# New orders for every engine of a two-layer linear-attention and MLP kernel, with the same operations

## The chip, the core and the metric

The kernel runs on one NeuronCore of a Trainium2 chip. The core has five engines with an instruction queue each: TensorE (PE, matmuls), VectorE (DVE), ScalarE (ACT), GpSimd (POOL) and SyncE (SP, which here only issues DMAs). An engine works its queue off in order; between engines there are semaphores. The metric is the time on the device for one execution, in microseconds (us).

## The reference

The input is x, 2048 tokens of 512 features in bfloat16. One set of weights is used twice, in two layers. A layer is a linear attention of 32 heads of 16 features, and then an MLP of 1792 hidden features with its own inner layer norm:

```
phi = lambda t: jnp.where(t > 0, t + 1, jnp.exp(t)) + 1e-6
pq, pk = phi(q), phi(k)
kv = jnp.einsum("bhsd,bhse->bhde", pk, v)
z = jnp.einsum("bhsd->bhd", pk)
num = jnp.einsum("bhqd,bhde->bhqe", pq, kv)
den = jnp.einsum("bhqd,bhd->bhq", pq, z)[..., None] + 1e-6
...
x = x + _A_ref(_layernorm(x, axis=-1), A_wqkv, A_wo)
x = x + _B_ref(_layernorm(x, axis=-1), B_w1, B_b1, B_w2, B_b2)
x = x + _A_ref(_layernorm(x, axis=-1), A_wqkv, A_wo)
x = x + _B_ref(_layernorm(x, axis=-1), B_w1, B_b1, B_w2, B_b2)
```

`_A_ref` is num / den times wo; `_B_ref` normalizes once more, multiplies by w1, adds b1, applies gelu, multiplies by w2 and adds b2. All tokens' keys are needed before the first token's attention is known, since kv and z are sums over the sequence.

## The kernel before, in words

The tokens are cut into four chunks c of four tiles k of 128 tokens; st = 4c + k numbers the tiles, L the layers. `build_kernel` does not issue instructions: it records operations into a graph (`G.op`), each with a name, an engine, and what it reads and writes. Names carry layer and tile. The ones that matter here:

- loads: x0 and x1 (first chunk), xc1, xc2, xc3 (the others), wka to wkd and wq (parts of the weights); b2 loads the bias of the second MLP matmul for all partitions.
- layer norm of tile st before the attention (A) or the MLP (B): statsA0_st and aggr (DVE), veps (one small operation, DVE or POOL), pow (POOL: the reciprocal root), norm (DVE, or ACT, which also takes nmr on POOL). The normalized tile is transposed: TA0_st, TB0_st are DMA transposes on SP's queue (L812); PTA0_2 and PTA0_3 are done by TensorE (L825) and copied by ACT (tcA0_2, tcA0_3, L835).
- K0_st, Q0_c_k: key and query matmuls (L879, L896, L909), four instructions each. phi of them: exp and relu on ACT, min on DVE, and the sum phi on DVE or POOL.
- G0_st: the running sum of y-transposed times phi(k) over tiles (L984 in layer 0, L1013 in layer 1); Z and zs, zb, ZR: the sum z. KV, kvm, M, cpm: the sum times wv, masked to its heads, times wo.
- Dividing by den: D, ln, rec, pr for chunk 0; for the others pz (query times z, L1077), red, den, rec, pr (L1089), and then TP0_c_k, a DMA transpose (L1093).
- WO0_st: the attention's output matmul (L1123); RA0_st adds the residual (DVE, L1128); b20_st adds the MLP's output bias to the residual ahead of time (L1139).
- W10_c_ft_h: the first MLP matmul for 128 hidden features (L1153), on 512 tokens, or in chunk 0 in two halves of 256; gelu0_c_ft_h on ACT (L1158). W20_st_0 and W20_st_7: the second MLP matmul in two parts of seven instructions (L1190); RB0_st adds the residual (L1196, or L1200 in the last layer, where OD stores the tile).
- warm0 to warm8: matmuls on ones ahead of the first real work (L749), 7 of 512 and 8 of 256 columns.

Layer 1 has the same names with 1 for 0. What runs when is not decided by a scheduler at build time: `CONF["ORDER"]` lists, for each engine, all its operations by name in the order in which they are issued, and `CONF["PLACES"]` says which buffer every tile has and who has it after whom (eight PSUM banks, and rings of SBUF buffers). `CONF["WAY"]` chooses the engine where there is a choice. `Settled` replays these lists, and `assign_waits` puts in the semaphore waits that the dependencies need: an operation waits for what it reads, and for the last user of the buffer that it takes over.

Of the kernel before, what the change touches and what calls it, by code (L numbers as in the profile page):

```python
# [185 lines left out]
def assign_waits(graph, order, sems, dma_sems):  # L186
# [10 lines left out]
    while len(done) < total:  # L197
        moved = False
        for e in ENGINES:
# [43 lines left out]
    LOADS=[['x0', 'sp', 'x', 0, 0, 1, ''], ['x1', 'sp', 'x', 0, 1, 4, ''], ['wkb', 'act', 'wk', 0, 2, 3, 'ones'], ['wka', 'sp', 'wk', 0, 0, 1, ''], ['wkd', 'act', 'wk', 0, 3, 4, ''], ['wkc', 'sp', 'wk', 0, 1, 2, ''], ['xc1', 'sp', 'x', 1, 0, 4, 'x0'], ['wq', 'sp', 'wq', 0, 0, 4, ''], ['xc3', 'sp', 'x', 3, 0, 4, ''], ['xc2', 'sp', 'x', 2, 0, 4, '']],  # L243
    ORDER={
        "sp":
            "x0 x1 wka wkc xc1 wq xc3 TA0_0 TA0_1 xc2 TA0_5 TA0_4 TA0_7 TA0_6 TA0_13 TA0_14 TA0_15 TA0_12 TA0_8 TA0_10 TA0_9 "
            "TA0_11 b1 Tb1 TP0_1_3 b2 TP0_1_1 TP0_1_0 TP0_1_2 TB0_0 TB0_1 TB0_2 TB0_3 TB0_7 TP0_2_1 TB0_5 TB0_4 TB0_6 TP0_2_2 "
            "TP0_2_0 TP0_2_3 TP0_3_2 TP0_3_0 TP0_3_1 TB0_10 TA1_0 TP0_3_3 TB0_8 TB0_9 TB0_11 TA1_1 TB0_12 TB0_14 TB0_15 "
            "TB0_13 TA1_2 TA1_3 TA1_7 TA1_4 TA1_6 TA1_5 TA1_9 TA1_8 TA1_11 TA1_10 TA1_13 TA1_12 TA1_15 TA1_14 TP1_1_2 TP1_1_0 "
            "TP1_1_1 TB1_0 TB1_1 TB1_2 TB1_3 TP1_1_3 TP1_3_1 TB1_6 TB1_4 TB1_5 TB1_7 TP1_3_3 TP1_2_1 TP1_3_0 TP1_3_2 TB1_13 "  # L250
# [3 lines left out]
            "warm0 warm8 warm2 warm6 PTC0 warm1 warm7 warm5 warm4 warm3 K0_0a K0_0b PTC1 K0_0c K0_0d PTA0_2 K0_1 PTA0_3 K0_2 "  # L254
            "K0_3 G0_0_0 G0_1_0 Q0_0_2 Q0_0_1 Q0_0_0 K0_5 G0_2_0 K0_4 Z0_0 G0_3_0 Q0_1_0 K0_7 Q0_1_3 K0_6 G0_4_0 G0_5_0 "
            "Q0_1_2 K0_13 K0_14 G0_6_0 K0_12 Z0_1 K0_15 K0_10 K0_8 K0_9 K0_11 G0_7_0 Q0_1_1 Z0_3 Q0_0_3 Z0_2 G0_8_0 G0_9_0 "
            "D0_0_2 G0_10_0 D0_0_0 G0_11_0 ZR0 D0_0_3 G0_12_0 G0_13_0 G0_14_0 G0_15_2 G0_15_1 G0_15_0 D0_0_1 Q0_3_3 G0_15_3 "
            "Q0_2_0 KV0_0 KV0_1 KV0_2 KV0_3 Q0_2_1 M0_2 M0_0 M0_1 Q0_2_2 M0_3 Q0_2_3 WO0_0_0 WO0_0_1 WO0_0_2 WO0_0_3 WO0_1_0 "
            "Q0_3_0 WO0_2_0 WO0_3_0 Q0_3_1 WO0_7_0 Q0_3_2 WO0_4_0 WO0_6_0 WO0_5_0 W10_0_3_0 W10_0_6_0 W10_0_1_0 W10_0_4_0 "
            "W10_0_0_0 W10_0_8_0 W10_0_12_0 W10_0_2_0 W10_0_7_0 W10_0_13_0 W10_0_5_0 W10_0_11_0 W10_0_9_0 W20_1_0 W10_0_10_0 "  # L260
            "W20_0_0 W10_0_9_1 W10_0_2_1 W10_0_4_1 W10_0_12_1 W20_0_7 W20_1_7 W10_0_6_1 W10_0_10_1 W10_0_8_1 W10_0_11_1 "
            "W10_0_1_1 WO0_9_0 W10_0_13_1 W10_0_5_1 W10_1_3_0 W10_1_9_0 W10_1_8_0 W10_1_2_0 W10_1_13_0 W10_0_7_1 W10_1_5_0 "
            "W10_1_1_0 W10_1_12_0 W10_1_4_0 W10_1_7_0 WO0_10_0 W10_1_0_0 W10_1_10_0 W10_0_0_1 W10_1_11_0 W10_1_6_0 WO0_8_0 "
            "WO0_11_0 W20_4_0 W20_7_0 W20_4_7 W20_7_7 W20_6_0 WO0_14_0 W10_0_3_1 WO0_12_0 W20_5_0 W20_6_7 WO0_13_0 K1_0 "
            "W20_5_7 WO0_15_0 W20_2_0 W20_2_7 W10_2_3_0 W10_2_10_0 W10_2_11_0 W10_2_0_0 W10_2_5_0 W20_3_0 W10_2_12_0 "
            "W10_2_4_0 W10_2_1_0 W20_3_7 W10_2_2_0 W10_2_6_0 W10_2_7_0 W10_2_13_0 W10_3_6_0 W20_10_0 K1_1 W10_3_7_0 W10_2_8_0 "
            "W10_3_13_0 W10_3_11_0 W10_2_9_0 W10_3_4_0 W10_3_9_0 W20_9_0 W20_9_7 K1_7 K1_2 K1_3 W10_3_5_0 W20_8_0 W20_10_7 "
            "W20_8_7 W10_3_12_0 W10_3_1_0 K1_6 W10_3_3_0 W20_11_0 W10_3_0_0 K1_4 K1_5 G1_0_3 W20_11_7 W10_3_2_0 W10_3_10_0 "
            "G1_0_1 G1_0_2 W10_3_8_0 G1_0_0 K1_9 W20_13_0 K1_8 W20_12_0 Q1_1_0 W20_12_7 W20_13_7 W20_14_0 W20_14_7 K1_11 "
            "K1_10 W20_15_0 W20_15_7 G1_1_3 G1_1_1 G1_1_0 G1_1_2 Q1_1_1 Q1_1_2 Q1_0_0 K1_12 K1_13 K1_15 K1_14 Q1_1_3 ZH "  # L270
            "G1_2_1 G1_2_2 Q1_0_3 Z1_3 Q1_0_2 Q1_0_1 G1_3_1 ZR1 D1_0_0 G1_3_2 G1_2_3 G1_2_0 D1_0_2 D1_0_1 G1_3_0 G1_3_3 "
            "Q1_3_1 D1_0_3 Q1_3_2 KV1_0 KV1_1 KV1_2 KV1_3 Q1_3_0 M1_2 M1_0 M1_1 M1_3 Q1_2_0 WO1_0_0 WO1_0_1 WO1_0_2 WO1_0_3 "
            "WO1_1_0 Q1_3_3 WO1_2_0 WO1_3_0 Q1_2_1 Q1_2_3 Q1_2_2 WO1_6_0 WO1_5_0 WO1_4_0 W11_0_12_0 W11_0_11_0 W11_0_6_0 "
            "W11_0_8_0 W11_0_2_0 W11_0_7_0 W11_0_1_0 W11_0_0_0 W11_0_10_0 W11_0_4_0 W11_0_9_0 W11_0_13_0 W11_0_5_0 W11_0_3_0 "
            "W11_0_0_1 W11_0_12_1 W11_0_6_1 W11_0_1_1 W11_0_5_1 W11_0_11_1 W11_0_4_1 W11_0_7_1 W11_0_8_1 W11_0_10_1 "
            "W11_0_13_1 WO1_7_0 W11_0_9_1 W11_0_3_1 W11_0_2_1 W21_0_0 W21_3_0 WO1_13_0 W21_0_7 W21_2_0 W21_2_7 W21_1_0 "
            "W21_1_7 WO1_15_0 W21_3_7 W11_1_12_0 W11_1_5_0 W11_1_1_0 WO1_9_0 W11_1_10_0 W11_1_6_0 W11_1_13_0 W11_1_2_0 "
# [12 lines left out]
            "expq0_2_0 ln0_0_1 rec0_0_1 cpm0_0 cpm0_1 cpm0_3 reluq0_3_3 expq0_3_3 expq0_2_2 expq0_2_1 expq0_2_3 reluq0_2_2 "  # L290
            "reluq0_2_1 expq0_3_0 b1c reluq0_2_3 reluq0_3_0 gelu0_0_6_0 gelu0_0_3_0 gelu0_0_1_0 gelu0_0_0_0 gelu0_0_8_0 "
            "gelu0_0_4_0 gelu0_0_12_0 gelu0_0_7_0 gelu0_0_2_0 gelu0_0_5_0 reluq0_3_1 gelu0_0_13_0 normB0_7 gelu0_0_9_0 "
            "gelu0_0_10_0 gelu0_0_11_0 expq0_3_1 expq0_3_2 normB0_6 gelu0_0_9_1 gelu0_0_4_1 gelu0_0_12_1 gelu0_0_6_1 "
            "gelu0_0_10_1 gelu0_0_2_1 gelu0_0_8_1 gelu0_0_11_1 gelu0_0_13_1 gelu0_0_5_1 gelu0_1_3_0 gelu0_1_9_0 gelu0_1_8_0 "
            "gelu0_0_1_1 gelu0_1_13_0 gelu0_0_7_1 gelu0_1_5_0 gelu0_1_1_0 gelu0_1_12_0 gelu0_1_2_0 gelu0_1_7_0 gelu0_1_4_0 "
            "gelu0_0_0_1 gelu0_1_0_0 gelu0_1_11_0 gelu0_1_10_0 gelu0_1_6_0 gelu0_0_3_1 normB0_11 normB0_9 expk1_0 reluk1_0 "
            "gelu0_2_10_0 gelu0_2_3_0 gelu0_2_5_0 gelu0_2_11_0 gelu0_2_12_0 gelu0_2_4_0 gelu0_2_0_0 gelu0_2_2_0 gelu0_2_6_0 "
            "gelu0_2_1_0 gelu0_2_13_0 gelu0_3_6_0 normA1_2 gelu0_3_7_0 gelu0_2_7_0 gelu0_3_13_0 gelu0_3_11_0 gelu0_2_8_0 "
            "normA1_7 gelu0_2_9_0 gelu0_3_4_0 expk1_2 expk1_7 expk1_3 normA1_6 reluk1_2 expk1_1 reluk1_3 normA1_5 gelu0_3_9_0 "
            "gelu0_3_5_0 gelu0_3_12_0 gelu0_3_3_0 gelu0_3_1_0 reluk1_6 expk1_6 reluk1_4 expk1_5 expk1_4 reluk1_7 normA1_9 "  # L300
            "gelu0_3_10_0 gelu0_3_2_0 gelu0_3_0_0 normA1_11 gelu0_3_8_0 expk1_8 normA1_10 reluk1_9 expk1_9 reluk1_8 expq1_1_0 "
# [1058 lines left out]
```

## Time and profile before

| | us |
|---|---|
| time, median of 3 runs | 323.07 (322.53 to 324.76) |
| time of the profiled execution | 323.1 |
| its span, first to last instruction | 321.9 |
| TensorE busy | 318.0 |
| DVE busy | 218.1 |
| ACT busy | 189.3 |
| POOL busy | 145.5 |

The table's lower half is from the profiled execution: the span is what the profiler saw of the program's instructions, and the execution took 1.2 us more than that. Busy times are unions of an engine's instructions. A matmul's end is modelled: a 512-column matmul is shown as 379 ns, while the next one of a row of such starts 216 ns after it, so that TensorE's pace is read from starts. DMAs belong to no engine's busy time; their landing is told by semaphores. "Margin" in this document means the time from the end of the last thing that an operation waits for to its start.

### The profile page before, as it was taken

The numbers are of one execution on the slowest core, as the hardware profiler recorded it, in microseconds if no ns is written. First come the engines' busy times: TensorE is split into PE (matmuls) and PEld (weight loads), VectorE is DVE, ScalarE is ACT, GpSimd is POOL, SyncE is SP. The second block draws the span as 40 slices with busy tenths as digits, with TensorE's granted clock in tenths as the row PEclk, the third lists the DMA queues.
The fourth block names the chain that finished last, engine by engine and source line by source line (L and its number), as shares of the span: only waits on it lengthen the run. The fifth ranks groups of instructions, "written<-read, shape, count | busy, mean of one in ns | idle before, by whom it ended". The sixth has DMA issues, their size and how long they took to land.

```text
span 321.9 us, 4748 instructions
## 1 busy us (share of the span) xinstructions
PE 318.0 (99%) x1703; PEld 157.4 (49%) x1703; DVE 218.1 (68%) x529; ACT 189.3 (59%) x324; POOL 145.5 (45%) x216
## 2 busy tenths in 40 slices
PE   8999999999999999999999999999999999999997
PEld 3444554666444444444444444558544444444444
DVE  5998789999786774028848899999889881101103
ACT  5898656797730636667962367979634442663320
POOL 6573978688655355101822415887454163000000
DMA  7844793142121412111010200122232322201002
GB/s 257 200 81 85 241 348 85 35 82 36 33 49 34 82 33 51 34 33 32 18 40 10 51 16 0 35 51 52 50 62 54 98 65 67 49 0 35 16 33 65
DMA packets 52355, 21.68 MB, mean 67 GB/s; under 512 B 47532, under 2 KB 50860, under 8 KB 52332
## 3 DMA queue, kind: packets, MB, share of 16 engines
q1 hardware_dynamic: 50844, 16.37, 22.4%
q0 software_dynamic: 1056, 4.72, 4.3%
q10 hardware_dynamic: 432, 0.30, 0.3%
q8 instruction: 13, 0.21, 0.3%
q14 instruction: 10, 0.08, 0.1%
HBM read 8.00 MB, written 2.10 MB: 31 GB/s over the span
## 4 chain that ended last, share of the span: by engine, by line
PE 97%; DMA 2%; DVE 0%; issue 0%
PE ps L1153 30%; PE ps L1190 29%; PE ps L1123 9%; PE ps L879 8%; PE ps L896 6%; PE ps L984 4%; PE ps L1013 4%; DMA t<-in_A_x_dram 2%; PE ps L909 2%; PE ps L1176 1%; PE ps L970 1%; PE ps L1034 1%; PE ps L1057 1%; PE ps L1100 1%; DVE stats L775 0%; PE ps L1048 0%
## 5 line engine op out<-in xcount | busy, mean ns | idle before, releaser
L1158 ACT ACTIVATE gT<-ps,b1c 128x512 bf16<-128x512 f32 (+1 forms) x140 | 77.0, 601 | 68.7 <-PE ps L1153 68.1
L1153 PE MATMUL ps<-t,w 128*128 128x512 bf16 (+1 forms) x560 | 102.5, 336 | 0.0
L1190 PE MATMUL ps<-w,gT 128*128 128x512 bf16 x434 | 98.6, 379 | 0.0
L1153 PEld LDWEIGHTS ps<-t,w 128*128 128x128 bf16 x560 | 54.8, 98 | 43.7 <-ACT gT L1158 0.2
L1190 PEld LDWEIGHTS ps<-w,gT 128*128 128x128 bf16 x434 | 42.5, 98 | 50.4
L784 POOL TENSOR_TENSOR rstd<-veps,neghalf 128x1 f32<-128x1 f32 x64 | 39.0, 625 | 41.1 <-DVE veps L782 38.9
L847 ACT ACTIVATE eb<-ps 128x512 bf16<-128x512 f32 x62 | 35.4, 606 | 19.3 <-PE ps L896 7.3
L1200 DVE TENSOR_TENSOR yb<-ps,xsb 128x512 bf16<-128x512 f32 x15 | 10.2, 688 | 41.4 <-PE ps L1190 41.4
L775 DVE BATCH_NORM_STATS2 stats<-xsb 128x6 f32<-128x512 f32 x48 | 32.0, 681 | 0.3
L1123 PE MATMUL ps<-gtb,t 128*128 128x512 bf16 x128 | 31.4, 379 | 0.0
L879 PE MATMUL ps<-wqkv,t 128*128 128x512 bf16 x128 | 30.9, 379 | 0.3 <-ACT t L835 0.3
L858 ACT ACTIVATE rb<-ps 128x512 bf16<-128x512 f32 x43 | 25.3, 607 | 5.8 <-PE ps L879 5.8
L798 ACT ACTIVATE yb<-xsb,nmr,rstd 128x512 bf16<-128x512 f32 x21 | 16.9, 814 | 15.1 <-POOL nmr L795 15.1
L896 PE MATMUL ps<-wqkv,t 128*128 128x512 bf16 x96 | 24.1, 379 | 0.0
L1089 POOL TENSOR_TENSOR t<-t,rr 128x512 bf16<-128x512 bf16 x18 | 19.3, 1072 | 9.0 <-DVE rr L1085 6.4
L782 POOL TENSOR_SCALAR veps<-mv 128x1 f32<-128x1 f32 x35 | 8.2, 236 | 32.7 <-DVE mv L777 31.3
L1196 DVE TENSOR_TENSOR xsb<-ps,xsb 128x512 f32<-128x512 f32 x16 | 10.8, 678 | 17.9 <-PE ps L1190 17.9
L1139 POOL TENSOR_TENSOR xsb<-xsb,b2b 128x512 f32<-128x512 f32 x17 | 21.4, 1267 | 3.0 <-DVE yb L803 2.9
L1077 POOL TENSOR_TENSOR lr<-t,zrow 128x512 f32<-128x512 bf16 x14 | 16.5, 1179 | 7.3 <-ACT zrow L997 4.5
L1123 PEld LDWEIGHTS ps<-gtb,t 128*128 128x128 bf16 x128 | 12.5, 98 | 14.5
L803 DVE TENSOR_SCALAR yb<-xsb,mv,rstd 128x512 bf16<-128x512 f32 x27 | 14.5, 542 | 7.3 <-POOL rstd L784 6.0
L879 PEld LDWEIGHTS ps<-wqkv,t 128*128 128x128 bf16 x128 | 12.1, 98 | 14.7 <-ACT t L835 0.9
(99 smaller groups left out, 363.7 us busy)
## 6 DMA issues: line engine op xcount, KB each, us to landing
w<-in_B_w_dram POOLq DMA_DIRECT2D x4, 896.0 KB, 9.1
out_dram<-yb SPq DMA_DIRECT2D x15, 128.0 KB, 2.0
t<-in_A_x_dram SPq DMA_DIRECT2D x3, 512.0 KB, 4.8
t<-yb SPq DMA_TRANSPOSE x62, 2.5
wqkv<-in_A_wqkv_dram SPq DMA_DIRECT2D x1, 512.0 KB, 5.9
wqkv<-in_A_wqkv_dram POOLq DMA_DIRECT2D x1, 512.0 KB, 4.7
wo<-in_A_wo_dram POOLq DMA_DIRECT2D x1, 512.0 KB, 5.3
t<-in_A_x_dram SPq DMA_DIRECT2D x1, 384.0 KB, 3.3
```

Source lines behind the costliest of these rows:

```text
L775: G.op("dve", lambda e: e.bn_stats(stats[:, s.slot, :], src()), 620, reads=src_keys, writes=[k + "s"], tiles=[s, *src_tiles], name=f"stats ...
L784: G.op("pool", lambda e: e.tensor_tensor(rstd[:, s.slot:s.slot + 1], veps[:, s.slot:s.slot + 1], neghalf[:], op=ALU.pow), 570, reads=[k + ...
L847: G.op("act", lambda e: e.activation(eb[:, et.slot, :], bank(bt), ACT.Exp, scale=by()), 478, reads=[src_key, *more_keys], writes=[f"e{tag} ...
L858: G.op("act", lambda e: e.activation(rb[:, rt.slot, :], bank(bt), ACT.Relu, scale=by()), 478, reads=[src_key, *more_keys], writes=[f"r{tag ...
L879: ins = e.matmul(bank(b), lhsT=yTa(yT)[:, dt, k * P:(k + 1) * P], rhs=wqkv[:, dt, D:2 * D], start=(i == 0 and n == 0), stop=(i == len(part ...
L896: ins = e.matmul(bank(b), lhsT=yTa(yT)[:, dt, k * P:(k + 1) * P], rhs=wqkv[:, dt, 0:D], start=(dt == 0), stop=(dt == DT - 1))
L1089: lambda e, d=d, tok=tok, heads=heads: e.tensor_tensor(heads(tok()), heads(tok()), rr[:, d.slot, :].unsqueeze(2).broadcast_to([P, H, DH]), ...
L1123: ins = e.matmul(bank(wb), lhsT=yTa(pq)[:, kt, k * P:(k + 1) * P], rhs=gtb[:, kt, :], start=(kt == 0), stop=(kt == DT - 1))
L1139: G.op("pool" if on_pool else "dve", lambda e: e.tensor_tensor(xsb[:, st, :], xsb[:, st, :], b2b[:], op=ALU.add), 1120 if on_pool else 600 ...
L1153: ins = e.matmul(bank(b, n), lhsT=w1[:, dt, ft * P:(ft + 1) * P], rhs=yTa(yT)[:, dt, k0 * P:k1 * P], start=(dt == 0), stop=(dt == DT - 1))
L1158: G.op("act", lambda e, ft=ft, b=b, k0=k0, k1=k1, n=n: e.activation(gT[:, g.slot, ft * 512 + k0 * P:ft * 512 + k1 * P], bank(b, n), ACT.Ge ...
L1190: ins = e.matmul(bank(b), lhsT=gT[:, g.slot, ft * 512 + k * P:ft * 512 + (k + 1) * P], rhs=w2[:, ft, :], start=(ft == 0), stop=(ft == FT - 1))
```

## The change

All five lists of `ORDER` are new, with `PLACES` to match, and 50 entries of `WAY`, each of which sends a small operation to the other one of DVE and POOL. Loads, warm-up matmuls and all operations are the same; TensorE, ACT and SP have the same operations in another order (389, 311 and 113 of them). DVE has 543 instead of 529 and POOL 198 instead of 212. The change was described as orders chosen anew "under a wide spread of the head's landings", that is of the times at which the first loads arrive, with "instruction packets placed by counting TensorE's instructions": the choice of the orders took into account where the DMA packets fall that bring in instructions. Neither of the two shows in the program except in the orders.

The first part of the lists, before (-) and after (+):

```diff
         "sp":
-            "x0 x1 wka wkc xc1 wq xc3 TA0_0 TA0_1 xc2 TA0_5 TA0_4 TA0_7 TA0_6 TA0_13 TA0_14 TA0_15 TA0_12 TA0_8 TA0_10 TA0_9 "
-            "TA0_11 b1 Tb1 TP0_1_3 b2 TP0_1_1 TP0_1_0 TP0_1_2 TB0_0 TB0_1 TB0_2 TB0_3 TB0_7 TP0_2_1 TB0_5 TB0_4 TB0_6 TP0_2_2 "
+            "x0 x1 wka wkc xc1 wq xc3 TA0_0 TA0_1 TA0_5 TA0_4 xc2 TA0_7 TA0_6 TA0_13 TA0_14 TA0_12 TA0_15 TA0_8 TA0_10 TA0_9 "
+            "TA0_11 b1 Tb1 TP0_1_3 TP0_1_1 TP0_1_0 TP0_1_2 TB0_0 TB0_1 TB0_2 b2 TB0_3 TB0_7 TB0_5 TB0_6 TB0_4 TP0_2_1 TP0_2_2 "
...
         "pe":
-            "warm0 warm8 warm2 warm6 PTC0 warm1 warm7 warm5 warm4 warm3 K0_0a K0_0b PTC1 K0_0c K0_0d PTA0_2 K0_1 PTA0_3 K0_2 "
-            "K0_3 G0_0_0 G0_1_0 Q0_0_2 Q0_0_1 Q0_0_0 K0_5 G0_2_0 K0_4 Z0_0 G0_3_0 Q0_1_0 K0_7 Q0_1_3 K0_6 G0_4_0 G0_5_0 "
+            "warm0 warm6 PTC0 warm1 warm7 warm4 warm8 warm3 warm5 warm2 K0_0a K0_0b PTC1 K0_0c K0_0d PTA0_2 K0_1 K0_2 PTA0_3 "
+            "G0_0_0 K0_3 G0_1_0 Q0_0_1 Q0_0_0 K0_5 Q0_0_2 K0_4 G0_2_0 Q0_1_0 G0_3_0 K0_7 G0_4_0 Q0_1_3 G0_5_0 K0_6 Z0_0 K0_13 "
...
         "act":
-            "wkb wkd sumA0_3 tcC0 sqA0_3 tcC1 reluk0_0 tcA0_2 expk0_0 tcA0_3 expk0_1 reluk0_1 reluk0_3 expk0_2 reluk0_2 "
+            "wkb wkd sumA0_3 tcC0 sqA0_3 tcC1 expk0_0 tcA0_2 reluk0_0 expk0_1 reluk0_1 tcA0_3 expk0_2 reluk0_3 reluk0_2 "
```

The change also adds to `CONF` one line, the order of the chunks, which is the old one, and rewrites the functions that took the chunks in their natural order to take it from there. A third way to divide by den (half of a chunk by features, half by tokens) and a half-tile load come into the code, but no entry of `WAY` or `LOADS` asks for them:

```diff
+    CHUNKS=[[0, 1, 2, 3], [0, 1, 2, 3], [0, 1, 2, 3]],
...
-        def by_token(L, c):
-            return eng(f"den{L}_{c}") == "tok"
+        def by_token(L, c, k=0):
+            way = eng(f"den{L}_{c}")
+            return way == "tok" or (way == "half" and k >= 2)
...
-        def mlp_up(L, c, yT, g):
+        def mlp_up(L, c, yT, g, first):
-            parts = [(0, 2), (2, 4)] if c == 0 else [(0, 4)]
+            parts = [(0, 2), (2, 4)] if first else [(0, 4)]
```

From WO1_9_0 on, 244.6 us into the run before, TensorE's list is the old one; ACT's, DVE's, POOL's and SP's follow from about the same point.

Of the 50 operations that change engines, these go from POOL to DVE: pz0_3_0, pz0_3_2, pz1_3_0, pz1_3_1; b20_0, b20_3, b20_4, b20_6, b20_8, b20_11, b20_13, b21_1; pr0_2_0, pr0_2_2, pr0_3_2, pr1_1_2, pr1_3_3; za3, za9; and 13 veps. From DVE to POOL go pz0_2_0, pz1_2_2, pz1_3_2, pz1_3_3; pr0_2_3, pr1_3_0; b21_0; za2, za8, za10; and 8 veps.

## The prediction

> **What bounds the kernel now.** I read the page first: its busy times and the shares of the chain that ended last.
>
> ```profile
> span 321.9 us, 4748 instructions
> PE 318.0 (99%) x1703; PEld 157.4 (49%) x1703; DVE 218.1 (68%) x529; ACT 189.3 (59%) x324; POOL 145.5 (45%) x216
> ...
> PE 97%; DMA 2%; DVE 0%; issue 0%
> ```
>
> TensorE is the bound, and everything else is late only if TensorE sees it. So the second view is who TensorE waited for, over the whole span:
>
> ```profile
> PE ps L749 <- PEq L1345: 0.8, 1, 0.8
> PE ps L825 <- DVE yb L803: 0.5, 1, 0.5
> PE ps L879 <- ACT t L835: 0.3, 1, 0.3
> PE ps L825 <- DVE yb L789: 0.2, 1, 0.2
> ```
>
> That is 1.8 us in all, every bit of it before 9.4 us. Going through TensorE's instructions one by one, 512-column matmuls start 0.216 us apart (eight take 1.73 us in the chain) and 256-column ones 0.109 us apart, without a gap from 9.39 to 319.70 us. So there is nothing to win behind the head. Ahead of it only warm-up matmuls run (0.83 to 4.61 us, until the first x tile has landed and been centred), and behind it stand the last DVE add and store (319.9 to 321.9). The third view is TensorE's timeline in the head:
>
> ```profile
> 7.67 1.03 PE L879 MATMUL ps<-wqkv,t 128*128 128x512 bf16 x4
> 9.16 0.40 PE L825 MATMUL ps<-idp,yb 128*128 128x128 bf16 x4 [0.47 <-DVE yb L803]
> 9.39 1.89 PE L879 MATMUL ps<-wqkv,t 128*128 128x512 bf16 x8
> 11.12 1.89 PE L984 MATMUL ps<-pkb,yb 128*128 128x512 bf16 x8
> ```
>
> The transpose at 9.16 (PTA0_3) stands in the queue ahead of K0_2, whose operand was ready at 8.65: 0.63 us are lost there.
>
> The margins behind the head are thin, though. I set each TensorE operation's start against the end of the last thing it needs: 66 of them have under 0.5 us (a gelu freeing a PSUM bank leaves 0.20 us again and again). The old order has no stall, but a new one with the same work can have some.
>
> **The change, part by part.** Every TensorE, ACT and SP operation stays, with its engine, and warm-up and loads too. 211 of TensorE's 389 places change, 203 of ACT's 311, 36 of SP's 113. 32 small operations go from POOL to DVE and 18 from DVE to POOL.
>
> (1) *The head.* Durations are those of the old rows, 0.06 us from an end to the waiter's start. Now K0_2 stands ahead of PTA0_3: it starts when tcA0_2 is done (8.65), at 8.71, issues until 9.57, and PTA0_3 follows at once until 9.80. G0_0_0 now stands ahead of K0_3 and needs phik0_0, done at 10.74 in the old run. It comes sooner: on ACT expk0_0 now precedes tcA0_2 (7.48 to 8.17), reluk0_0 follows (8.53 to 9.2); on DVE mink0_0 moves ahead of normA0_3 (8.70), normA0_3 ends 9.4, phik0_0 at 9.77. So G0_0_0 9.83 to 10.69. K0_3 needs tcA0_3, now behind expk0_1 and reluk0_1 on ACT (10.06 to 10.68): 10.74 to 11.60. G0_1_0 needs phik0_1 (11.36, behind normA0_5): 11.60 to 12.45. In the old run G0_1_0's last issue ended at 12.85. So **-0.40 us**. Bounds: -0.63 (that wait gone and nothing new) and +0.53 (phik0_0 no sooner than 10.74, then three operations of 0.86 from 10.80). I take -0.40, as each term is a row.
>
> (2) *The next loads.* SP now sends TA0_5 and TA0_4 ahead of xc2. In the old run TA0_5, sent 0.7 us behind xc2, took 3.70 us, and landed 15.14. Now it goes at 11.04 and lands near 13.5 (2.5 us, as the undisturbed ones), for K0_5 at 14.18; TA0_4 near 14.9 for K0_4 at 15.9. xc2 is sent some 2.5 us later and lands near 17.5, and statsA0_8, its first reader, stands on DVE at about 17.8. Its transpose leaves after 25 in both. Nothing is lost: 0.
>
> (3) *Instruction packets.* Transposes in this kernel land 2.4 to 2.5 us after their issue, save a few. The view of the transposing line from 16 to 24 us, and of the queues from 17 to 22 us:
>
> ```profile
> DMA to landing us min/median/max: 2.4/2.5/4.1
> ...
> q8 instruction: 1, 0.02, 1.6%
> q14 instruction: 1, 0.01, 1.0%
> ```
>
> The 4.1 is TA0_6 (17.70 to 21.76): a 16 KB packet of queue 8 began at 18.05 and took 1.26 us. The same befell TA1_13 (4.01, packet at 179.04) and TP1_3_0 (4.02, packet at 243.26); an 8 KB packet of queue 14 cost TB1_0 and TB1_2 0.85 us each. So a hit costs a transpose 1.55 or 0.85 us. There are 13 queue-8 packets, 110 to 149 matmuls apart; TensorE's instructions keep their number, so by that count they stay where they are to within the 0.4 us of (1). TA0_6 is hit again, sent at about 16.8 and landing near 20.9; its reader K0_6 moved from 21.89 (margin 0.13 in the old run) to 22.8. TB0_1 landed at 59.50, and a packet began at 59.56; DVE's minq0_2_2 leaves its way, so it is no later. W10_1 starts at 76.1 instead of 78.3, but its transposes lose TP0_2_1 from between them, the last lands near 73.9. I take 0; a hit without cover is at most +1.55.
>
> The Trainium skill, "Runtime: NRT & Kernel Launch", section "Instruction fetch mechanics", says that instructions come in 16 KiB blocks of 256 by a DMA queue and that crossing a block is mostly hidden. By that the term would be 0 wherever packets fall; the rows agree on the size and show 1.55 us on three transposes.
>
> (4) *DVE from 64 to 96 us.* Nine wide operations come to DVE here (b20_0, _3, _4, _6, pz0_3_0, pz0_3_2, pr0_2_0, pr0_2_2, pr0_3_2) and two wide and two small ones leave: 7 x 0.69 - 0.28 = +4.55 us. DVE has 32.00 - 27.84 = 4.16 us free there:
>
> ```profile
> 64.00:72.00 8.00, 8.00 (x60) 5.54 (x58) 7.51 (x19) 7.41 (x15) 6.99 (x11) 1.00 0.40 82
> 72.00:80.00 8.00, 8.00 (x52) 4.99 (x51) 7.93 (x16) 6.28 (x13) 6.56 (x5) 1.00 0.20 36
> 80.00:88.00 8.00, 8.00 (x40) 3.82 (x39) 6.27 (x15) 5.92 (x11) 5.47 (x6) 1.00 0.16 33
> 88.00:96.00 8.00, 8.00 (x41) 3.83 (x40) 6.14 (x17) 3.61 (x7) 3.95 (x5) 1.00 0.24 49
> ```
>
> (The third busy time is DVE's.) Adding the rows up in the new order from normB0_5 at 68.47: RB0_0 ends 77.9 (WO0_9 needs its bank at 80.9), pr0_2_2 80.2 (with its transpose 82.7; WO0_10 at 85.6), pr0_2_0 86.7 (89.1; WO0_8 at 92.1). Tight is RA0_8, which frees the bank of W20_7_0, due at 95.34: with three long rows of the old run kept (1.30, 0.97 and 1.56 us from start to next start) RA0_8 ends at 95.66, +0.37; with 0.65 for each it ends at 93.9 as before, 0. Taken: **+0.20**, as POOL has less to do beside it.
>
> (5) *Start of layer 1's MLP.* pr1_1_2 comes to DVE ahead of RA1_0, but fills 205.9 to 206.6, and RA1_0 waits for WO1_0_3 until 206.65 anyway. vepsB1_1 goes to POOL, 0.24 instead of 0.15, so TB1_1 is about 0.1 later of the 0.57 that W11_0 has. 0; +0.4 if the 8 KB packet (0.85) hits TB1_1 instead of TB1_0. From WO1_9_0 on (244.6 us) TensorE's list is the old one: 0.
>
> Sum: 323.1 (profiled execution: span 321.9 and 1.2 around it; the median is 323.07, the same) - 0.40 + 0.20 = **322.9 us**.
>
> **Rivals.**
> A, the forecast: 322.9. Own range 322.2 (-0.63, and the 0.3 by which runs lie lower) to 324.4 (+0.53, +0.37, +0.4).
> B, thin margins become waits: one place hit by a packet without cover, as TB0_1 would be if 0.1 us later (1.55 - 0.96 of margin = 0.6), and a gelu chain or two (0.2 to 0.5 each): +1.5, 324.4. For it: the 66 margins; against it: the old order had the same and no stall.
> C, slower than before: DVE's two-input operations blocked by POOL's.
>
> ```profile
> 74.22 2.61 DVE L1077 TENSOR_TENSOR lr<-t,zrow 128x512 f32<-128x512 bf16 x2
> ...
> 79.27 1.37 DVE L1139 TENSOR_TENSOR xsb<-xsb,b2b 128x512 f32<-128x512 f32 x1
> ```
>
> Both stand beside POOL's b20 additions; alone they take 0.68. A blocked one costs up to 0.97. RA0_8 can lose 1.4 us before W20_7_0 waits. Five of the nine moved ones blocked: 4.85 - 1.4 = +3.4, 326.3. The Trainium skill, "SBUF — State Buffer", section "Who interferes with whom", says that a DVE instruction with two SBUF inputs and a GpSimd one that reads SBUF shut each other out for a whole instruction; the trace agrees for these two. Against C: of the 32 DVE operations of these three kinds 5 were long (0.98 to 1.64), and POOL has nine fewer to collide with.
> D, the clock: matmuls start 0.427 us apart until 4.2 us and 0.216 after 4.84. Two of three warm-ups ahead of PTC0 move behind it, so TensorE idles 0.63 instead of 0.15 us there. If the doubling came later, eight matmuls of K0_0 and K0_1 would cost 0.21 more each, half of it in waits: +0.8, 323.7. The Trainium skill, "TensorE: Matmul & The Clock Gate", section "What's actually happening", has a free-running window of 3413 ns of activity; no run here shows its threshold.
>
> **How the numbers follow.** Chances: A 0.66, B 0.20, C 0.07, D 0.07. Range 322.2 to 325.4, which leaves out C and the ends of A and B. One per cent (3.2 us) is about what a measurement of this kernel can tell. Faster by more would need 3.2 us, and all of TensorE's waits are 1.8: 0.01. Slower by more is C and B's far end: 0.08. Within: 0.91.
>
> **What would show it.** Step 1: G0_1_0's last issue near 12.45 and no wait before PTA0_3. Step 3: long transposes only at TA0_6, TA1_13, TP1_3_0 or others with no TensorE wait behind. Step 4: DVE full from 64 to 96, W20_7_0 on time. TensorE's waits should again be under 2.5 us in all. I am wrong if waits for ACT's gelu or DMA stand in that list behind 10 us.

## The result and the profile after

The changed kernel is slower: a median of 324.59 us (324.01 to 326.01) against 323.41 us (322.53 to 325.58) for the kernel before, 17 executions each, ratio 1.0043 with a 95% interval of 1.0030 to 1.0056. That is 1.4 us (1.0 to 1.8) by the ratio and 1.2 by the medians, inside the predicted range and on the other side of the forecast: slower, where faster was forecast. The profiled execution took 324.15 us (323.1 before), its span 322.9 (321.9).

The page of the changed kernel, with the lines that stand against those of before:

```profile
span 322.9 us, 4718 instructions
...
PE 317.3 (98%) x1673; PEld 157.2 (49%) x1703; DVE 224.1 (69%) x543; ACT 191.2 (59%) x326; POOL 132.4 (41%) x202
...
PE 84%; DVE 9%; ACT 2%; POOL 2%; issue 1%; DMA 1%; SPq 0%
```

TensorE is still the bound, but the chain that ended last now runs through DVE for 9% of the span: somewhere TensorE waited for DVE. (30 of its 1703 matmul records are missing, one every 10.8 us; a gap of exactly one matmul's pace is such a record and no idle time.) The whole list of TensorE's waits says where:

```profile
PE ps L759 <- PEq L1373: 0.8, 1, 0.8
PE ps L841 <- DVE yb L805: 0.4, 1, 0.4
PE ps L1149 <- DVE xsb L1154: 0.4, 1, 0.4
PE ps L1216 <- DVE veps L798: 0.3, 1, 0.3
```

The first two stand in the head. The third and fourth are new and stand at 54.8 and 234.7 us. The list counts from the modelled end of the matmul ahead, and the next one could have started before that end; so I take idle time from matmul starts: 0.52 us ahead of WO0_2_0 (plus 0.05 ahead of WO0_3_0), 0.41 ahead of W21_2_0, and 0.14 and 0.04 ahead of W11_0_9_0 and W11_0_13_0, which the list doesn't have. In all 1.17 us behind the head; the kernel before had none in its profile.

**First wait, 54.8 us.** DVE's timeline in the changed kernel (start, duration, line and operation; L867 is the min, the old L851):

```profile
49.92 0.32 DVE L1126 TENSOR_SCALAR rd<-rd 128x32 f32<-128x32 f32 x1
50.15 1.21 DVE L867 TENSOR_SCALAR eb<-eb 128x512 bf16<-128x512 bf16 x1
51.28 0.34 DVE L1128 RECIPROCAL rr<-rd 128x32 f32<-128x32 f32 x1
51.55 0.62 DVE L869 SCALAR_TENSOR_TENSOR t<-ps,eb 128x512 bf16<-128x512 f32 x1
```

and POOL's timeline in the changed kernel at that time:

```profile
49.03 1.17 POOL L1102 TENSOR_TENSOR t<-t,lr 128x512 bf16<-128x512 bf16 x1
50.15 1.06 POOL L1132 TENSOR_TENSOR t<-t,rr 128x512 bf16<-128x512 bf16 x1
```

minq0_2_0 took 1.21 us instead of 0.28: it ended 0.15 us after POOL's pr0_1_1, which began in the same moment. In the kernel before the min came first. DVE's line of it, and POOL's pr0_1_1:

```profile
50.36 0.28 DVE L851 TENSOR_SCALAR eb<-eb 128x512 bf16<-128x512 bf16 x1
50.41 1.14 POOL L1089 TENSOR_TENSOR t<-t,rr 128x512 bf16<-128x512 bf16 x1
```

Behind the min RA0_1 ended at 54.78 instead of 54.11, and WO0_2_0, which in the new `PLACES` takes the bank that RA0_1 frees, was due at 54.32.

**The wait at 234.7 us**, the last in order of time. DVE's timeline of the changed kernel again; L819 is normB1_5 (0.54 before), the last line RA1_13, whose bank W21_2_0 takes (the veps of the list begins beside it and is not what TensorE needs):

```profile
232.35 1.44 DVE L819 TENSOR_SCALAR yb<-xsb,mv,rstd 128x512 bf16<-128x512 f32 x1
233.72 0.34 DVE L1128 RECIPROCAL rr<-rd 128x32 f32<-128x32 f32 x1
233.98 0.62 DVE L1154 TENSOR_TENSOR xsb<-ps,xsb 128x512 f32<-128x512 f32 x1
```

POOL's pz1_2_2, which the change took from DVE, ran from 232.36 to 233.51. W21_2_0 takes RA1_13's bank in the kernel before too; there RA1_13 ended at 232.99 and W21_2_0 began at 233.60.

**The wait at 215.7 us**, between the other two in time. Here POOL is the one shut out. nmrB1_1 in POOL's timeline of the changed kernel (0.65 in the kernel before, 0.27 in the median of its kind):

```profile
211.28 1.09 POOL L811 TENSOR_SCALAR nmr<-mv,rstd 128x1 f32<-128x1 f32 x1
```

and, in DVE's timeline of the changed kernel, phiq1_3_2, minq1_3_1 and phiq1_3_0 beside it:

```profile
211.29 0.42 DVE L880 TENSOR_TENSOR t<-eb,rb 128x512 bf16<-128x512 bf16 x1
211.62 0.29 DVE L876 TENSOR_SCALAR eb<-eb 128x512 bf16<-128x512 bf16 x1
211.83 0.42 DVE L880 TENSOR_TENSOR t<-eb,rb 128x512 bf16<-128x512 bf16 x1
```

Behind it normB1_1 starts at 212.41, and the transpose TB1_1 lands at 215.65 (214.55 before) for W11_0_9_0.

So all three are collisions of short DVE and POOL operations. Lengthened operations are not more than before: among operations of the same kind and shapes, 14 of DVE's lie 0.25 us or more above the median before and 13 after, by 6.2 and 7.2 us in all; of POOL's 17 and 16, by 7.2 and 6.9. Three of them now fall where nothing is left to hide them.

### The profile page after: what moved, and what is told of

The parts are those of the page before. It is cut to its first block, busy times and chain, and to the rows that moved or that the text cites. A ratio compares the mean times of both kernels' runs of the same rounds, so it can differ in the third digit from the quotient of the medians.

```text
span 322.9 us, 4718 instructions
## 1 busy us (share of the span) xinstructions
PE 317.3 (98%) x1673; PEld 157.2 (49%) x1703; DVE 224.1 (69%) x543; ACT 191.2 (59%) x326; POOL 132.4 (41%) x202
## 4 chain that ended last, share of the span: by engine, by line
PE 84%; DVE 9%; ACT 2%; POOL 2%; issue 1%; DMA 1%; SPq 0%
PE ps L1179 30%; PE ps L1216 26%; PE ps L1149 7%; PE ps L895 6%; PE ps L1034 4%; PE ps L928 4%; PE ps L1005 2%; POOL rstd L800 1%; PE ps L916 1%; DVE stats L791 1%; DVE rd L1123 1%; DMA t<-in_A_x_dram 1%; PE ps L1202 1%; DVE gtb L1021 1%; ACT yb L814 1%
## 5 line engine op out<-in xcount | busy, mean ns | idle before, releaser
L1216 PE MATMUL ps<-w,gT 128*128 128x512 bf16 x423 | 97.5, 379 | 0.8 <-DVE veps L798 0.3
L800 POOL TENSOR_TENSOR rstd<-veps,neghalf 128x1 f32<-128x1 f32 x64 | 38.3, 606 | 23.0 <-DVE veps L798 21.4
L798 POOL TENSOR_SCALAR veps<-mv 128x1 f32<-128x1 f32 x30 | 7.0, 234 | 52.8 <-DVE mv L793 50.8
L1132 POOL TENSOR_TENSOR t<-t,rr 128x512 bf16<-128x512 bf16 x15 | 16.7, 1113 | 8.2 <-DVE rr L1128 8.1
L1165 DVE TENSOR_TENSOR xsb<-xsb,b2b 128x512 f32<-128x512 f32 x22 | 16.0, 731 | 4.6 <-ACT yb L814 4.6
```

Of the source, the lines that this page charges most:

```text
L800: G.op("pool", lambda e: e.tensor_tensor(rstd[:, s.slot:s.slot + 1], veps[:, s.slot:s.slot + 1], neghalf[:], op=ALU.pow), 570, reads=[k + ...
L1216: ins = e.matmul(bank(b), lhsT=gT[:, g.slot, ft * 512 + k * P:ft * 512 + (k + 1) * P], rhs=w2[:, ft, :], start=(ft == 0), stop=(ft == FT - 1))
```

## The experiments

Theory L: these three collisions are the loss. The rivals were that the new bank places make the waits whatever DVE does (B), that the transposes are late by themselves (P), and that the loss is spread over head, clock and packets (S). All experiments are edits of `ORDER` (one of `WAY` too); the diffs show the tokens that move.

**f1_min**, on DVE:

```diff
- kvm0_3 rec0_1_1 cpm0_2 red0_1_2 den0_1_0 minq0_2_0 rec0_1_0
+ kvm0_3 cpm0_2 red0_1_2 den0_1_0 minq0_2_0 rec0_1_1 rec0_1_0
```

> The changed kernel with one operation moved on DVE: rec0_1_1, whose end releases POOL's pr0_1_1, stands behind minq0_2_0 instead of ahead of cpm0_2. Theory L (short DVE operations shut out by a POOL operation that begins in the same moment, at three places without margin): minq0_2_0 falls from 1.21 to 0.3-0.6 us, RA0_1 ends before 54.2 instead of at 54.78, the 0.52 us in which TensorE waits for it ahead of WO0_2_0 go, and the kernel ends 0.5 us earlier, near 323.65 by one profiled execution (324.15 now); the two later waits (0.14 at W11_0_9_0, 0.41 at W21_2_0) stay, though a shift of 0.5 us may move them. Rival B (the new places of the PSUM banks and TensorE's new list make the wait whatever DVE does): minq0_2_0 gets short, yet WO0_2_0 still waits 0.3 us or more and the end stays at 324.1.

Measured: 323.63 us, ratio to the kernel before 1.0009 (0.9993 to 1.0025); profiled 323.62. DVE's min, in the timeline of this run:

```profile
50.19 0.28 DVE L867 TENSOR_SCALAR eb<-eb 128x512 bf16<-128x512 bf16 x1
```

and POOL's pr0_1_1 and pr0_1_0 in it:

```profile
50.81 2.07 POOL L1132 TENSOR_TENSOR t<-t,rr 128x512 bf16<-128x512 bf16 x2 [0.58 <-DVE rr L1128]
```

The min begins as before the edit but nothing of POOL's begins with it; RA0_1 ends at 54.00 and the wait is gone with the banks unchanged. Rival B falls for this place.

**f2_nmr**, on DVE:

```diff
- RA1_2 phiq1_3_2 minq1_3_1 phiq1_3_0 RA1_3
+ RA1_2 RA1_3 phiq1_3_2 minq1_3_1 phiq1_3_0
```

> The changed kernel with RA1_3 ahead of phiq1_3_2, minq1_3_1 and phiq1_3_0 on DVE, so that POOL's nmrB1_1 begins beside an addition that reads PSUM. Theory L: nmrB1_1 falls from 1.10 to 0.3 us, normB1_1 starts near 211.6 instead of 212.41, TB1_1 lands near 214.9 instead of 215.65, and the wait ahead of W11_0_9_0 (0.14 us, and 0.04 at W11_0_13_0) goes: 0.15 us less than the changed kernel, 324.0. Rival P (the transpose itself is late, by an instruction packet): nmrB1_1 is short, but TB1_1 takes over 3 us and W11_0_9_0 still waits.

Measured: 324.12 us in the one execution. POOL's nmrB1_1 in this run:

```profile
211.44 0.27 POOL L811 TENSOR_SCALAR nmr<-mv,rstd 128x1 f32<-128x1 f32 x1
```

It took 0.27 us beside the addition from PSUM, normB1_1's transpose landed at 214.98, and the waits of 0.14 and 0.04 are gone; the other two stand. As L has it; TB1_1 took 2.40 us from issue to landing, so rival P falls.

**f3_ra** and **fix3**. f3_ra, on DVE:

```diff
- den1_3_3 normB1_5 rec1_3_3 RA1_13
+ den1_3_3 RA1_13 normB1_5 rec1_3_3
```

> The changed kernel with RA1_13 ahead of normB1_5 on DVE. Theory L: normB1_5 is still shut out by a POOL operation (over 1 us), but now behind RA1_13, which ends by 233.7 instead of 234.60; the 0.41 us ahead of W21_2_0 go, and the kernel ends 0.4 us earlier, 323.75. Rival B (TensorE's new list asks for that bank too early, whatever stands ahead of the addition): W21_2_0 still waits 0.2 us or more, since WO1_13_0 itself ends at 232.90.

> The changed kernel with all three edits. Theory L: no wait of TensorE behind 12 us over 0.1 us, the end 1.0 to 1.1 us earlier than the changed kernel's, 323.05 by one profiled execution, and the ratio to the kernel before between 0.9985 and 1.0005 (the head keeps its gain of 0.15 us). Rival S (the loss is spread: clock in the head, landings, packets): the kernel stays 0.5 us or more slower than before, ratio 1.0015 or more. Rival M (new ties elsewhere, as every operation behind 55 us comes 0.5 us earlier): the three waits go and others of 0.2 to 0.5 us stand in their place.

Measured: f3_ra 324.51 us in one execution, fix3 323.55, ratio 1.0015 (1.0001 to 1.0028). The list of TensorE's waits in f3_ra, without its first line:

```profile
PE ps L1149 <- DMA t<-t: 0.5, 1, 0.5
PE ps L841 <- DVE yb L805: 0.4, 1, 0.4
PE ps L1149 <- DVE xsb L1154: 0.4, 1, 0.4
```

The wait ahead of W21_2_0 is gone, and the first line is a new one: 0.63 us ahead of WO1_15_0 (241.06), for the transpose TP1_3_3. In its new place RA1_13 waits for WO1_13_0 and DVE idles 0.5 us; DVE works without a pause from there to pr1_3_3, which feeds that transpose. In the changed kernel the transpose had landed only 0.38 us ahead of WO1_15_0; now it lands later, and TensorE, no longer held up at W21_2_0, comes to it sooner. fix3 has this wait (0.62) and no other. Rival M came true, by a lengthened DVE chain: the ratio alone would fit rival S too, but the wait in the trace is M's sign.

**fix5** and **fix5_again**: all three edits, and

```diff
 dve
- red1_2_1 RB1_0 pz1_2_0 pr1_3_3
+ red1_2_1 pr1_3_3 RB1_0 pz1_2_0
 act
- expk0_1 reluk0_1 tcA0_3
+ expk0_1 tcA0_3 reluk0_1
```

> All three edits of the run before, and two more: on DVE pr1_3_3 stands ahead of RB1_0 and pz1_2_0 (the last run had a new wait of 0.62 us ahead of WO1_15_0, for the transpose TP1_3_3 that pr1_3_3 feeds), and on ACT tcA0_3 stands ahead of reluk0_1. Theory L, with the addition that the wait at WO1_15_0 came from the DVE chain that my third edit had lengthened by 0.5 us (DVE idle ahead of RA1_13): TP1_3_3 lands near 238.2, the 0.62 us go, no wait of TensorE behind 12 us is over 0.1 us; tcA0_3 ends 0.2 us earlier against its operand and the wait ahead of K0_3 falls from 0.26 to about 0.05, of which G0_1_0 keeps 0.05 to 0.1. The time is 322.85 to 323.0, beside 322.9 of the kernel before: ratio 0.9985 to 1.0010. Rival S (a spread loss): no wait is left, yet the ratio stays 1.0015 or more. Rival M: another wait of 0.3 us or more takes its place.

> The changed kernel with the five edits, a second time, since its first profile fell on an execution in which x1 landed 1.1 us late. Theory L: with x1 at 4.5 to 4.8 us the waits behind 14 us are 0.1 us or less in all (the 0.18 ahead of K0_7 belonged to the late landing), the stretch from G0_1_0's last issue to TensorE's last is 306.9 to 307.0 us as in the kernel before, the time 322.8 to 323.1, and the ratio again between 0.998 and 1.001. Rival S (a loss without a wait in the trace): 1.0015 or more.

Measured: ratio 0.9999 (0.9980 to 1.0018), and the second time 1.0003 (0.9989 to 1.0018); medians 323.31 and 323.46, beside 322.99 and 323.12. The whole list of TensorE's waits in fix5_again:

```profile
PE ps L759 <- PEq L1373: 0.8, 1, 0.8
PE ps L841 <- DVE yb L805: 0.4, 1, 0.4
```

In fix5_again nothing is left behind the head. The first profile, fix5, in which x1 landed late, has 0.18 us ahead of K0_7, over the 0.1 that I had allowed, and 0.09 ahead of WO1_9_0; TP1_3_3 landed at 240.27 instead of near 238.2, yet in time. The kernel cannot be told from the one before. Rival S's sign (no wait left, ratio 1.0015 or more) did not come. But each interval by itself reaches 1.0018, and the plain medians lie 0.3 above in both, so a loss of some 0.3 us is not ruled out. The edit on ACT gave the head 0.09 us, in both runs.

**plant**: the kernel before, with the collision put in:

```diff
- kvm0_3 cpm0_2 red0_1_2 rec0_1_1 den0_1_0 minq0_2_0
+ kvm0_3 rec0_1_1 cpm0_2 red0_1_2 den0_1_0 minq0_2_0
```

> The kernel before with one DVE operation moved to where the changed kernel has it: rec0_1_1 ahead of cpm0_2, so that POOL's pr0_1_1 can begin at the moment when minq0_2_0 does. Theory L: minq0_2_0 is shut out and takes about 1.2 us (0.28 in the kernel before), RA0_1 ends some 0.7 us later (54.8 instead of 54.11), but the kernel before has the bank of q0_3_3 under WO0_2_0, so TensorE doesn't wait and the time stays (within 0.1 us by the trace). A stall needs the collision and the missing margin together. Rival B: with a collision alone TensorE waits 0.4 us or more. Rival N (no collision without the changed kernel's other moves): minq0_2_0 stays at 0.28.

Measured: 323.31 us in one execution. DVE's min in this run:

```profile
50.04 1.21 DVE L851 TENSOR_SCALAR eb<-eb 128x512 bf16<-128x512 bf16 x1
```

and WO0_1_0 in TensorE's timeline of it (the idle time in brackets leaves out the drain of the matmul ahead):

```profile
52.03 0.82 PE L1123 MATMUL ps<-gtb,t 128*128 128x512 bf16 x3 [0.35 <-DVE t L853]
```

One early operation on DVE suffices for the collision. My expectation of no wait was wrong: RA0_1 ended at 54.25 without harm, but phiq0_2_0, which stands directly behind the min, ended at 51.97 (51.36 before) and its bank belongs to WO0_1_0, which waited 0.51 us. I had looked at one reader of the delay only.

**pz_back**: the changed kernel with pz1_2_2 on DVE again.

```diff
 pool
- pz1_2_1 pz1_2_2 pr1_3_0
+ pz1_2_1 pr1_3_0
 dve
- pr1_3_3 red1_2_2
+ pr1_3_3 pz1_2_2 red1_2_2
```

> The changed kernel with the one operation given back to DVE whose move to POOL stands at the third wait: pz1_2_2, behind pr1_3_3 there. Theory L (any POOL operation that begins in the moment of normB1_5 shuts it out): POOL's next one, pr1_3_0, begins at 232.4 in its place, normB1_5 still takes 1.2 us or more, and W21_2_0 still waits 0.3 to 0.5 us. Rival W (the moved operation itself is the cause): normB1_5 takes 0.55 us, RA1_13 ends near 233.7 and the wait of 0.41 us goes.

Measured: 325.51 us in one execution (all is 1.1 us later, since x1 landed so late). DVE's normB1_5 in this run:

```profile
233.47 1.34 DVE L819 TENSOR_SCALAR yb<-xsb,mv,rstd 128x512 bf16<-128x512 f32 x1
```

and POOL's pr1_3_0:

```profile
233.48 1.06 POOL L1132 TENSOR_TENSOR t<-t,rr 128x512 bf16<-128x512 bf16 x1
```

W21_2_0 still waits 0.32 us. POOL works through a queue there, and whichever operation begins with the norm shuts it out; the moved one is not the cause in itself.

**head_old**: the changed kernel with the old head order.

```diff
 pe
- K0_1 K0_2 PTA0_3 G0_0_0 K0_3 G0_1_0
+ K0_1 PTA0_3 K0_2 K0_3 G0_0_0 G0_1_0
 act
- expk0_0 tcA0_2 reluk0_0 expk0_1 reluk0_1 tcA0_3
+ reluk0_0 tcA0_2 expk0_0 tcA0_3 expk0_1 reluk0_1
 dve
- normA0_1 statsA0_5 mink0_0 aggrA0_5 normA0_3 phik0_0 statsA0_4 mink0_1 aggrA0_4
+ statsA0_5 normA0_3 aggrA0_5 normA0_1 statsA0_4 mink0_0 aggrA0_4 phik0_0 mink0_1
```

> The changed kernel with the old order of its head up to G0_1_0: PTA0_3 ahead of K0_2 on TensorE, reluk0_0 and tcA0_3 at their old places on ACT, normA0_3 ahead of mink0_0 and normA0_1 on DVE; the warm-up keeps the new order. By the prediction's first step the last issue of G0_1_0, counted from the landing of x1, is 0.40 us later than in the changed kernel. By the two traces (12.85 before, 12.70 after) it is 0.15 us later: PTA0_3 waits 0.6 us ahead of K0_2 again, and the 0.18 and 0.26 us ahead of K0_2 and K0_3 go. If instead the warm-up's new order and TensorE's later clock doubling took the rest of the forecast gain (rival D), K0_0 starts over 0.1 us later after the landing of x1 than the 1.28 us of the kernel before.

Measured: 324.37 us in one execution. G0_1_0's last issue comes 8.01 us after the landing of x1, against 8.08 with the new head. The old head is a little shorter here, not longer; both expectations were wrong. (A new wait of 0.21 us ahead of the first W10 matmul stands behind it: an instruction packet fell on the transposes TB0_0 and TB0_1.) K0_0 starts 1.28 us after x1, so the warm-up takes nothing.

**norm_first** and **before_again** ask what the 0.63 us ahead of PTA0_3 in the old profile were. norm_first is the kernel before with

```diff
- normA0_2 statsA0_5 normA0_3 aggrA0_5
+ normA0_2 normA0_3 statsA0_5 aggrA0_5
```

> The kernel before with one DVE operation moved: normA0_3 ahead of statsA0_5. Theory H (the 0.63 us ahead of PTA0_3 in the profile of before are the landing of the load xc1 at 8.07 us, for which statsA0_5 waits, with normA0_3 queued behind it though its operands were there at 7.84): normA0_3 runs from 7.9 to 8.3, PTA0_3 follows K0_1 without a wait, and the last issue of G0_1_0 comes 7.80 to 7.85 us after the landing of x1 (8.27 in the profile of before, 7.93 in the run with rec0_1_1 moved, where xc1 landed at 7.72, and 8.08 in every run of the new head); no wait behind it. The time falls by 0.1 to 0.45 us beside the kernel before: ratio 0.9986 to 0.9997. Rival: PTA0_3's wait isn't xc1's; then the wait stays at 0.3 us or more, and the ratio at 1.000.

> The kernel before, unchanged, for a second profile. Theory H: the wait ahead of PTA0_3 is the landing of xc1 less about 7.45 us (0.63 with 8.07, 0.29 with 7.72), so the head (last issue of G0_1_0 after the landing of x1) is 7.9 to 8.4 and moves one to one with it, and the stretch from there to TensorE's last issue is 306.9 us, with no wait over 0.05 us. If the old head is always 8.27 whatever xc1 does, theory H is wrong.

Measured: norm_first 323.81 us, ratio 1.0019 (0.9997 to 1.0041), so no gain; before_again 324.63 in its one execution. TensorE's timeline in norm_first, with the end of K0_1 (8.13), the transpose PTA0_3 (8.56) and later K0_5 (15.43; the releaser named is not what it needed, TA0_5 landed last):

```profile
8.13 0.59 PE L879 MATMUL ps<-wqkv,t 128*128 128x512 bf16 x2
8.56 0.39 PE L825 MATMUL ps<-idp,yb 128*128 128x128 bf16 x4
...
15.43 0.38 PE L879 MATMUL ps<-wqkv,t 128*128 128x512 bf16 x1 [0.20 <-ACT yb L798]
```

PTA0_3 follows K0_1 without a wait and the head is 7.87 us, near what I expected; then 0.36 us are lost ahead of K0_5, whose transpose TA0_5 landed at 15.30, 4.0 us after its issue beside the load xc2. The median lies 0.6 above that of the kernel before, more than the trace explains; this stays open. In before_again the head is 7.79 us, below the 7.9 to 8.4 that I expected, and in the list of TensorE's waits stands one that the first profile of the same kernel hasn't, 0.85 us by starts, for TB0_1:

```profile
PE ps L1153 <- DMA t<-yb: 0.7, 1, 0.7
```

**norm_sp**: norm_first, and on SP

```diff
- TA0_1 xc2 TA0_5 TA0_4
+ TA0_1 TA0_5 xc2 TA0_4
```

> The kernel before with normA0_3 ahead of statsA0_5 on DVE, as in the run before, and the transpose TA0_5 ahead of the load xc2 on SP: the run before had a new wait of 0.36 us ahead of K0_5, whose transpose TA0_5 landed at 15.30, 4.0 us after its issue, beside xc2. Theory: TA0_5 lands near 13.8, the wait goes, the head keeps 7.80 to 7.87 us and the stretch behind it 306.9; 322.7 by one execution with x1 at 4.6, ratio 0.9985 to 1.0. Rival (the gain is eaten again, by xc2's later landing): K0_6 or K0_8 waits 0.3 us or more, and the ratio is 1.000 or above. Executions in which x1 lands 1.1 us late, or in which an instruction packet hits TB0_1 (0.85 us in the second profile of the kernel before), occur in both kernels and can hide 0.2 us.

Measured: 323.40 us, ratio 1.0002 (0.9984 to 1.0021). TA0_5 landed at 13.68 and K0_5 didn't wait, but TA0_4 landed at 16.88 beside xc2 and K0_4 waited 0.13, K0_6 0.11; the head took 7.93, 0.2 of it in matmuls at half pace. No kernel here beats the one before by what can be measured.

All profiles together. The head is the time from the landing of x1 to G0_1_0's last issue end, the rest runs from there to that of TensorE's last matmul, and the waits are TensorE's idle times over 0.03 us behind 14 us:

| kernel | profiled us | x1 lands | head | rest | waits | rest less waits |
|---|---|---|---|---|---|---|
| before | 323.10 | 4.58 | 8.27 | 306.91 | 0 | 306.91 |
| before_again | 324.63 | 5.72 | 7.79 | 307.77 | 0.85 | 306.92 |
| plant | 323.31 | 4.56 | 7.93 | 307.47 | 0.56 | 306.91 |
| norm_first | 323.08 | 4.61 | 7.87 | 307.26 | 0.36 | 306.90 |
| norm_sp | 323.07 | 4.64 | 7.93 | 307.13 | 0.24 | 306.89 |
| after | 324.15 | 4.62 | 8.08 | 308.12 | 1.17 | 306.95 |
| f1_min | 323.62 | 4.66 | 8.08 | 307.53 | 0.59 | 306.94 |
| f2_nmr | 324.12 | 4.77 | 8.08 | 307.92 | 0.99 | 306.93 |
| f3_ra | 324.51 | 4.77 | 8.08 | 308.31 | 1.38 | 306.93 |
| fix3 | 323.46 | 4.50 | 8.08 | 307.52 | 0.62 | 306.90 |
| fix5 | 324.26 | 5.74 | 7.99 | 307.19 | 0.26 | 306.93 |
| fix5_again | 323.46 | 5.20 | 7.99 | 306.93 | 0 | 306.93 |
| pz_back | 325.51 | 5.72 | 8.09 | 308.03 | 1.08 | 306.95 |
| head_old | 324.37 | 4.67 | 8.01 | 308.34 | 1.36 | 306.98 |

The last column is the same to 0.1 us. What differs between kernels and executions is when x1 lands, the head, and the waits; the waits are the change's loss.

## Why the prediction was wrong

The step that failed is the sum: it has no term for collisions at places that the change part by part never visited. In the two profiles the head ended 0.16 us sooner instead of 0.40, DVE from 64 to 96 us cost 0 instead of 0.20, and the waits, at nothing in the sum, took 1.17: 323.1 - 0.16 + 1.17 = 324.1, where 324.15 was measured. Two of the three waits (WO0_2_0, W21_2_0) are in none of my steps, and I had given that kind, a thin margin that becomes a wait, 0.20 as rival B, at 324.4 us. B was right in kind, not in its mechanism: I had priced a packet or gelu chains, so that its 324.4 lies near the measured 324.59 is luck. The mechanism stood in rival C, for other operations and another place.

**(1) The head, -0.40.** Two errors. The end of G0_1_0 was forecast at 12.45 and came at 12.69. TensorE's timeline of the changed kernel:

```profile
7.69 2.08 PE L895 MATMUL ps<-wqkv,t 128*128 128x512 bf16 x8
9.61 0.39 PE L841 MATMUL ps<-idp,yb 128*128 128x128 bf16 x4
9.84 1.03 PE L1005 MATMUL ps<-pkb,yb 128*128 128x512 bf16 x4
10.96 1.04 PE L895 MATMUL ps<-wqkv,t 128*128 128x512 bf16 x3
11.83 1.03 PE L1005 MATMUL ps<-pkb,yb 128*128 128x512 bf16 x4
```

K0_2 (8.74), PTA0_3 and G0_0_0 came within 0.04 us of the forecast, without a wait ahead of PTA0_3; K0_3 came at 10.96 instead of 10.74, since ACT's row of six operations ended tcA0_3 at 10.90, 0.22 later than I had added up. The larger error is the old side: its 0.63 us were no fixed cost. normA0_3's operands were there at 7.84, but it stood behind statsA0_5, which waited for the load xc1 (8.07). The old head was 8.27 us where xc1 landed 3.49 us after x1, 7.93 at 3.16, 8.01 at 3.24 (head_old) and 7.79 at 2.31: one to one above 7.8. The new head is 8.08 or 8.09 in all six profiles of it, with xc1 2.32 to 3.47 us after x1. So the change takes the dependence on xc1 away, and the four old heads average 8.00: the term was about 0, if anything a small loss.

**(2) The next loads, 0.** Right: TA0_5 landed at 13.34, TA0_4 at 14.82, xc2 at 17.27, each within 0.25 us of the forecast.

**(3) Packets, 0.** Right for the changed kernel: TA0_6, TA0_13 and TA0_14 took 4.97, 4.31 and 3.66 us beside a 16 KB packet, and no TensorE wait stands behind them. The size of a hit was too small, though: 2.5 us on TA0_6, not 1.55. What I wrote of TB0_1 as rival B's place happened in the kernel before: in before_again a packet that began at 59.66 fell on it (4.25 us from issue to landing), for 0.85 us of wait. In the first profile it began 0.06 us after TB0_1 had landed.

**(4) DVE from 64 to 96 us, +0.20.** The windows of the changed kernel (third busy time: DVE):

```profile
64.00:72.00 8.00, 7.95 (x59) 5.54 (x58) 7.40 (x19) 7.53 (x15) 5.26 (x11) 1.00 0.39 83
72.00:80.00 8.00, 7.95 (x51) 4.98 (x51) 7.96 (x19) 6.67 (x15) 0.00 (x0) 1.00 0.29 59
80.00:88.00 8.00, 7.95 (x42) 4.01 (x41) 6.20 (x15) 4.93 (x10) 3.57 (x4) 1.00 0.12 25
88.00:96.00 8.00, 8.00 (x40) 3.83 (x40) 7.50 (x19) 4.23 (x7) 3.98 (x6) 1.00 0.16 33
```

DVE is busy 29.07 us in the four, not 32. The nine operations came, but the ones that stand in these windows in both kernels took 2.4 us less in all. POOL is busy 12.8 us there instead of 23.0 and does nothing at all from 72 to 80, where the additions b20 on DVE take 0.69. RA0_8 ended at 94.30 and W20_7_0 started at 95.78, 1.48 us of margin: 0, the lower end.

**(5) Start of layer 1's MLP, 0.** Wrong place to stop: I priced vepsB1_1's move at 0.1 us, but TB1_1 landed 1.1 later (0.43 of that since TensorE was late by then, 0.45 the longer nmrB1_1, the rest smaller delays ahead of it), where 0.57 was the margin. Cost 0.18. **From WO1_9_0 on, 0:** right, no wait there.

**Rivals C and D.** Of C's nine operations one was shut out (pr0_2_0, 1.30 us), at no cost to TensorE. The Trainium skill, "SBUF — State Buffer", section "Who interferes with whom", says more than the half that I used: besides instructions with two SBUF inputs, a tensor_scalar in a two-port mode takes the shared pair as well, whoever issues first holds it for the whole instruction and the other fully blocks, and a tensor_reduce never takes it on trn2. The runs agree on who is shut out and for how long: a min until pr0_1_1 had ended (1.21), and the reductions below untouched. That the min runs in such a mode is not shown by a run. POOL's nmr waited for three DVE operations and not for one (1.09). On who issues first they can't tell where both begin within 0.01 us: normB1_5's recorded start lies 0.007 us ahead of pz1_2_2's, and it was shut out. Read whole, that rule would have sent me to every min and norm beside POOL. Of D, TensorE's pace did double later in the changed profile (5.3 against 4.2 us), but K0_0 starts 1.35 us after x1 there and 1.28 to 1.41 in all profiles, of both warm-up orders; the last matmul at half pace ended anywhere from 3.8 to 6.5 us, in either order. So its price was near 0.

Of my signs of being wrong, the waits behind 10 us came, but for DVE's additions rather than gelu or DMA.

## What to carry to other kernels

In a schedule without slack, a reordering with the same work had one price here: waits at places that it didn't mean to touch; so list the margins of the bound engine's operations, and for each that is thin, the whole chain behind it, with every operation that another engine can shut out. A stall seen in one profile is a term only if what it hangs on is fixed: look for the load or transfer that an in-order queue waits for, and for a second execution. When a wait is removed, look at what the edit itself delays: one of my three edits put back more than it took.

## What the runs showed of the hardware

Over all 14 profiles, DVE's operations that begin while a wide POOL operation (pr, pz, b2 or phi) has over 0.15 us left to run fall into two kinds. Unmoved: the reductions red (0.63 to 0.69 us in 155 cases), the additions RA from PSUM (0.62 to 0.69 in 148), statistics (0.63 to 0.70). Shut out until POOL's has ended: min, 0.42 to 1.25 instead of 0.28 in 38 cases; norm, 1.27 instead of 0.54 in the four that began 0.07 us after a pr; pr, pz and b2, up to 1.64 instead of 0.68. The lengths follow POOL's operation: a min ends 0.15 to 0.2 us after it (0.60 us with 0.45 left, 0.94 with 0.79, 1.25 with 1.10), and normB1_5 0.28 to 0.29 us after it, behind pz1_2_2 (1.16 left, 1.44), pr1_3_0 in pz_back (1.06, 1.34) and pr1_3_0 in fix5 (0.99, 1.27). A min beside which POOL's had 0.15 us or less left took its 0.28 to 0.30.

Where both began within 0.02 us of each other, the starts in the profile don't say who loses. In the three waits, plant and pz_back it was the shorter one, four times DVE's and once POOL's, where a row of three DVE operations shut it out. But in the kernel before POOL's addition b20_13 was the longer one and lost to DVE's za2, which began with it at 153.05: 1.68 us instead of 1.16.

The landing of x1 varied from 4.50 to 5.74 us, and TensorE's last matmul moved with it one to one. Instruction packets come within a few matmuls of a fixed place in TensorE's list, not exactly at it: in the changed kernel and its variants the one near 60 us came between about 12 matmuls ahead of the first W10 matmul (head_old) and that matmul itself (f2_nmr), and it cost the kernel before 0.85 us in before_again and head_old 0.21. The landing of x1 (+1.15), this packet (+0.85) and the head (-0.48) are the 1.5 us by which the two profiles of the kernel before differ. For the executions without a profile that is not shown. Landing and packet are both larger than the 0.1 to 0.3 us by which orders of the head differ.
